# Retention attention and a GELU feed-forward on one core: v of chunk 2 moved to SyncE's queue, casts of chunk 2's k blocks two tiles later

## The chip, the core and the metric

The kernel runs on one core of a Trainium2 chip. Five engines work on their own instruction streams and wait for each other by semaphores: PE (TensorE, matmuls), DVE (VectorE), ACT (ScalarE), POOL (GpSimd) and SP (SyncE, which here only issues DMAs). The metric is the device time of one execution in microseconds (us). Six executions of the kernel before took 213.31 to 215.12 us, median 214.15 us.

## What is computed

q, k and v are float32 of shape 4 x 8 x 768 x 64 (batches, heads, positions, width of a head). Each head keeps a 64 x 64 state that decays by a factor gamma of its own at each position:

```python
for t in range(S):
    state = gamma[None, :, None, None] * state + np.einsum('bhd,bhe->bhde', k[:, :, t], v[:, :, t])
    y[:, :, t] = scale * np.einsum('bhd,bhde->bhe', q[:, :, t], state)
```

The result, laid out as 3072 tokens of width 512, goes through a feed-forward layer: `h = x @ w_in` (512 to 2048), GELU in its tanh form, and `g @ w_out` (2048 to 512).

## The kernel before

**Chunks.** The 768 positions are cut into six chunks of 128 (c = 0 to 5). A chunk holds its 128 positions of all four batches, so 512 tokens. Within a chunk the recurrence is done as matrix products. For a batch b of chunk c the names in the code are: `mm_T`/`ev_T` make the transposed q and k (tile qkT), `mm_A`/`ev_A` the masked products of k and q (PE writes a_ps, DVE multiplies by the mask into a_sb, line 257), `mm_yc` and `mm_yi` the output (y_ps) from the state and from a_sb with v, `ev_Y` brings it into xT, and `mm_s`/`ev_S` update the state st. `att_T`, `att_S` and `att_AY` bundle these.

**Feed-forward.** `moe1` (one tile of 128 hidden channels by 512 tokens, four matmuls) and `moe1_two` (two tiles of channels by 256 tokens, eight matmuls) multiply xT by w_in into a bank h_ps (line 390), and ACT takes the GELU of it into g (line 406). There are two banks for h_ps, so PE can be two tiles ahead of ACT, and no more. The second product uses a Winograd-like scheme with seven products in place of eight: `w_sums` makes sums of weights, `g_sums` sums of g into the tiles s_g (four operations for one or two groups of rows, line 429; on POOL for chunks 1 to 4), and `units_w(c)` is a list of 14 units (seven products, two halves of the tokens each) of eight matmuls into o_ps (line 498). The fifth unit of the list (unit 4) is the first that reads s_g, all eight groups of s_g[2]. Units 11 and 13 end with the stores of the chunk's output, 512 KB each, issued by POOL (line 531).

**The order of the work is written out by hand.** `run(units, after)` issues the units one by one, and after unit i whatever `after[i]` lists. An engine executes its own instructions strictly in that order. Here the stage of chunk c with its `moe1` units is called M(c), and that with `units_w(c)` is W(c). M(1) is a `run` of 16 units of `moe1_two` (lines 784 to 806), W(1) a second one (lines 807 to 823). From chunk 2 on, M(c) and W(c) are one `run` of 16 + 14 units (lines 826 to 857). The attention of chunk c + 1 is slipped in between the units of chunk c.

**Transposes of q and k.** For chunks 2 to 5 q and k come into SBUF a second way as well: `load_blk` (line 106) loads a chunk in 16 DMAs of 64 KB as blocks of 32 x 32 (tiles q32 and kT32, pieces of 128 bytes), `prep_blk` casts one batch of it to float16 (line 172 on ACT, line 174 on POOL), and `ev_T` transposes it on DVE in one instruction (line 230). Each cast reads what all 16 DMAs wrote. q32 has two buffers, kT32 one. `load1` (line 100) loads one batch of q, k or v as rows (256 KB, pieces of 256 bytes); `prep1` casts and scales it (v on POOL, line 185; k on ACT, line 172). v32 and k32 have eight buffers each, taken in the order of the loads in the code.

**DMA issue.** `load(c)` (line 117) is what SP issues for chunk c: q blocks, v (for c > 2), k blocks, then the rows of k. `load(2)` stands at line 738, behind a DMA of a table (line 737) that waits for POOL's line 736; `load(3)` stands after unit 8 of M(1), `load(4)` after unit 0 of M(2), `load(5)` after unit 0 of M(3). v of chunk 2 is issued by POOL, after unit 6 of the run that does W(0) (line 771). The weights, most of chunk 1's q, k and v, and nearly all stores of the output are issued by POOL too. In the profile q0 (software_dynamic) is POOL's DMA queue and q1 (hardware_dynamic) is SP's.

**The casts of the k blocks.** For chunk 2 ACT does them: batches 0 and 1 after units 8 and 10 of M(1), batches 2 and 3 in W(1). For chunk 3 ACT does them after units 8, 9, 11 and 13 of M(2) (line 844). For chunks 4 and 5 POOL does all four at the end of W(2) and W(3), behind the stores (line 856), and ahead of the g_sums of the next chunk.

Of the kernel before, what the change touches and what calls it, by code (L numbers as in the profile page):

```python
# [16 lines left out]
def kernel(  # L17
# [9 lines left out]
    nc = tc.nc  # L27
    B, H, S, Dh = q.shape
# [52 lines left out]
    def ld_all(key):  # L81
        if key not in raw:
            raw[key] = ld.tile(
                [128, B * NHP, 4, 32],
                F32,
                tag=key[0],
                bufs=2 if key[0] == "q32" else 1,
                name=key[0],
            )
        return raw[key]  # L90

    def ld_tile(nm, c, b):
        if nm == "q":
            t = ld_all(("q32", c)).rearrange("p (b hp) a d -> p b (hp a d)", b=B)
            return t[:, b].rearrange("p (h d) -> p h d", h=H)
        if (nm, c, b) not in raw:
            raw[nm, c, b] = ld.tile([128, H, Dh], F32, tag=f"{nm}32", bufs=8, name=f"{nm}32")
        return raw[nm, c, b]

    def load1(eng, nm, c, b):  # L100
        eng.dma_start(  # L101
            out=ld_tile(nm, c, b),
            in_=srcs[nm][b, :, c * C:(c + 1) * C, :].rearrange("h p d -> p h d"),
        )

    def load_blk(nm, c):
        t = ld_all((nm + ("32" if nm == "q" else "T32"), c))
        src = srcs[nm].rearrange("b (hp j) s (dd d) -> j dd s (b hp) d", j=2, dd=2)
        for j in range(2):
            for dd in range(2):  # L110
                for a in range(4):
                    p0, t0 = (2 * j + dd) * 32, c * C + a * 32
                    nc.sync.dma_start(  # L113
                        out=t[p0:p0 + 32, :, a, :], in_=src[j, dd, t0:t0 + 32]
                    )

    def load(c):
        load_blk("q", c)
        if c > 2:
            for b in range(B):  # L120
                load1(nc.sync, "v", c, b)
        load_blk("k", c)
        for b in range(B):
            load1(nc.sync, "k", c, b)

# [528 lines left out]
    VE, AC, PO, SY = nc.vector, nc.scalar, nc.gpsimd, nc.sync  # L654
# [81 lines left out]
    nc.gpsimd.tensor_copy(out=dec[0:1, 0, 0:1], in_=w_out_sb[3][0:1, 0, 0:1])  # L736
    nc.sync.dma_start(out=dec.rearrange("p h t -> p (h t)"), in_=dec_h.ap())
    load(2)
    for nm, b in ("q3", "k3", "v2", "v3"):
        load1(PO, nm, 1, int(b))  # L740
# [19 lines left out]
    def mm_Y(b, tag):  # L760
# [7 lines left out]
            1: [(w_sums, 3)],  # L768
            3: [(prep_qk, 1, 0)],
            5: [(att_T, 1, 0), (prep1, PO, "v", 1, 0), (prep1, PO, "v", 1, 1)],  # L770
            6: [(prep_qk, 1, 1)] + [(load1, PO, "v", 2, b) for b in range(B)],
            7: [(att_1A, 0)],
            8: [(att_T, 1, 1)],
            9: [(prep_qk, 1, 2)],
# [20 lines left out]
            5: [(mm_Y, 3, "o"), (ev_Y, 1, 3)],  # L795
            7: [(g_sums, PO, 1, 4, 8, 0, 1)],
            6: [(att_S, 1, 3), (prep_blk, AC, "q", 2, 0)],
            8: [(prep_blk, AC, "k", 2, 0), (load, 3)],
            9: [(prep_blk, AC, "q", 2, 1)],
            10: [(att_T, 2, 0), (prep_blk, AC, "k", 2, 1)],  # L800
            11: [(g_sums, PO, 1, 0, 4, 1, 2)],
            12: [(att_T, 2, 1)],
            14: [(att_AY, 1, (), "o", 2, (0, 1), None), (prep1, PO, "v", 2, 0), (prep1, PO, "v", 2, 1)],
            15: [(g_sums, PO, 1, 4, 8, 1, 2), (prep1, PO, "v", 2, 2), (prep1, PO, "v", 2, 3)],
        },
    )
    run(
# [18 lines left out]
    for c in range(2, NCk):  # L826
# [24 lines left out]
        if m < NCk:  # L851
            more(0, (load, m))
            for b in range(B):
                more((20, 21, 23, 24)[b], (prep_blk, AC, "q", m, b))
                more(24, (prep1, PO, "v", m, b))
                more(29, (prep_blk, PO, "k", m, b))
# [31 lines left out]
```

## Time and profile before

| | us |
|---|---|
| median of six executions | 214.15 |
| the profiled execution | 215.12 |
| its span, first to last instruction | 213.1 |
| time around the span | 2.0 |
| PE busy | 199.8 (94% of the span) |
| POOL busy | 130.0 (61%) |
| DVE busy | 111.1 (52%) |
| ACT busy | 106.1 (50%) |

A timeline line gives the start, the duration, the engine, the line of the kernel, the operation, output and inputs by the program's names, and how many instructions were merged; in brackets stands how long the engine had been idle before it, and what ended that. For SP the lines are the issue of DMAs, so their duration is the time that issuing took, and data lands later (a median of 2.8 us after the issue for a k block, of 5.3 us for a batch of k rows on SP). A line of a waits view reads "engine line <- what it waited for: us in total, times, longest". The windows view gives for each stretch the busy time of each engine with the number of instructions in brackets, then the granted PE clock, the DMA engines' share and GB/s. The lines of DMA queues give packets, MB and share of the 16 DMA engines.

### The profile page before, as it was taken

What the parts mean: (1) busy time and instruction counts of PE and PEld (TensorE: products, weight loads), DVE (VectorE), ACT (ScalarE), POOL (GpSimd) and SP (SyncE); (2) the same over time, 40 slices, a digit from 0 to 9 for tenths busy, and PEclk for the clock granted to TensorE, in tenths of its full rate; (3) what the DMA queues carried; (4) which work ended last, traced back from release to release, by engine and by line L of the source; (5) the groups of instructions that cost most, each with busy time, mean ns of one, the idle gap of its engine ahead of it and who ended that gap; (6) DMA issues with size and microseconds to landing.
All of it is one profiled execution on the core that took longest, in us unless ns stands there. A gap on an engine that the chain in (4) does not pass through costs nothing.

```text
span 213.1 us, 4854 instructions
## 1 busy us (share of the span) xinstructions
PE 199.8 (94%) x1948; PEld 137.2 (64%) x1948; DVE 111.1 (52%) x230; ACT 106.1 (50%) x189; POOL 130.0 (61%) x136
## 2 busy tenths in 40 slices
PE   5789999999991999999999999999999999999993
PEld 1447747777781788854478844588844688644883
DVE  3336489488541288820768740657730956134421
ACT  2375575355453474457874156655166631367321
POOL 0599335956295699528999379999289991200000
PEclk9999999999998599999999999999999999999999
DMA  7999999999878879779879799697891000310005
GB/s 163 287 253 207 206 207 298 328 293 238 196 123 165 164 123 208 113 186 276 126 144 192 112 253 233 102 218 119 139 311 38 0 3 3 143 54 0 3 0 198
DMA packets 117302, 34.24 MB, mean 161 GB/s; under 512 B 109984, under 2 KB 114464, under 8 KB 117280
## 3 DMA queue, kind: packets, MB, share of 16 engines
q1 hardware_dynamic: 103808, 18.21, 45.3%
q0 software_dynamic: 6944, 13.63, 24.2%
q10 hardware_dynamic: 6528, 2.10, 3.9%
q8 instruction: 15, 0.25, 0.5%
q14 instruction: 7, 0.06, 0.1%
HBM read 31.83 MB, written 6.29 MB: 179 GB/s over the span
## 4 chain that ended last, share of the span: by engine, by line
PE 66%; SPq 13%; DMA 11%; DVE 3%; POOL 3%; issue 1%; ACT 1%; ACTq 0%
PE h_ps L390 30%; PE o_ps L498 29%; SPq L113 12%; DMA w_out<-in_moe_w_out_dram 6%; DMA k<-in_k_dram 3%; PE y_ps L281 2%; PE y_ps L268 2%; PE a_ps L244 2%; DVE t_w L429 2%; DMA kT<-in_k_dram 2%; DVE s_g L429 1%; POOL w_in L371 1%; POOL k L185 1%; SPq L101 1%; PE s_ps L305 1%
## 5 line engine op out<-in xcount | busy, mean ns | idle before, releaser
L390 PE MATMUL h_ps<-xT,w_in 128*128 128x512 f16 (+2 forms) x488 | 90.2, 342 | 4.9 <-ACT g L406 4.9
L406 ACT ACTIVATE g<-h_ps 128x512 f16<-128x512 f32 (+1 forms) x98 | 57.4, 588 | 35.1 <-PE h_ps L390 34.6
L390 PEld LDWEIGHTS <-w_in 128*128 128x128 f16 x488 | 46.8, 100 | 43.2 <-issue 7.4
L257 DVE TENSOR_TENSOR a_sb<-a_ps,mask 128x512 f16<-128x512 f32 x48 | 30.1, 684 | 27.8 <-PE a_ps L244 27.8
L429 POOL TENSOR_TENSOR s_g<-g 128x512 f16<-128x512 f16 x32 | 36.9, 1152 | 12.4 <-ACT g L406 12.4
L498 PEld LDWEIGHTS <-s_g 128*128 128x128 f16 x320 | 30.2, 98 | 4.3
L498 PE MATMUL o_ps<-t_w,s_g 128*128 128x256 f16 x240 | 27.8, 273 | 0.0
L498 PEld LDWEIGHTS <-g 128*128 128x128 f16 x240 | 23.5, 98 | 3.5
L230 DVE STREAM_TRANSPOSE qkT<-kT 128x512 f16<-128x512 f16 x16 | 10.9, 683 | 21.3 <-ACT kT L172 15.7
L185 POOL TENSOR_TENSOR v<-v,cst 128x512 f16<-128x512 f32 x20 | 20.3, 1040 | 0.0
L429 POOL TENSOR_TENSOR s_g<-s_g,g 128x512 f16<-128x512 f16 x16 | 18.5, 1153 | 1.3
L429 POOL TENSOR_TENSOR s_g<-g,s_g 128x512 f16<-128x512 f16 x16 | 18.4, 1153 | 0.0
L531 POOL DMA_DIRECT2D out_dram<-o_sb x8 | 5.9, 736 | 20.5 <-DVE o_sb L429 16.9
L498 PE MATMUL o_ps<-w_out,g 128*128 128x256 f16 x160 | 18.3, 273 | 0.0
L297 DVE TENSOR_TENSOR xT<-y_ps,dec 128x512 f16<-128x512 f32 x20 | 13.1, 687 | 6.3 <-PE y_ps L281 6.3
L527 ACT COPY o_sb<-o_ps 128x512 f32<-128x512 f32 (+1 forms) x5 | 2.7, 543 | 25.0 <-PE o_ps L498 25.0
L429 DVE TENSOR_TENSOR s_g<-g 128x512 f16<-128x512 f16 x16 | 6.7, 421 | 12.6 <-ACT g L406 12.6
L172 ACT CAST q<-q 128x512 f16<-128x512 f32 x20 | 12.0, 619 | 2.4 <-DMA q<-in_q_dram 2.4
L172 ACT CAST k<-k 128x512 f16<-128x512 f32 x20 | 11.6, 619 | 0.1
L230 DVE STREAM_TRANSPOSE qkT<-q 128x512 f16<-128x512 f16 x16 | 11.1, 692 | 0.8 <-ACT q L172 0.7
L322 DVE SCALAR_TENSOR_TENSOR st<-st,cst,s_ps 128x128 f16<-128x128 f16 (+1 forms) x40 | 10.0, 316 | 0.5 <-PE s_ps L305 0.5
L521 ACT COPY s_u<-o_ps 128x512 f32<-128x512 f32 (+1 forms) x6 | 3.1, 514 | 14.2 <-PE o_ps L498 7.4
(68 smaller groups left out, 207.3 us busy)
## 6 DMA issues: line engine op xcount, KB each, us to landing
out_dram<-o_sb POOLq DMA_DIRECT2D x10, 512.0 KB, 4.8
k<-in_k_dram SPq DMA_DIRECT2D x18, 256.0 KB, 5.3
q<-in_q_dram SPq DMA_DIRECT2D x64, 64.0 KB, 3.0
kT<-in_k_dram SPq DMA_DIRECT2D x64, 64.0 KB, 2.8
v<-in_v_dram SPq DMA_DIRECT2D x14, 256.0 KB, 4.2
w_in<-in_moe_w_in_dram POOLq DMA_DIRECT2D x4, 512.0 KB, 8.7
w_out<-in_moe_w_out_dram POOLq DMA_DIRECT2D x4, 512.0 KB, 13.9
v<-in_v_dram POOLq DMA_DIRECT2D x8, 256.0 KB, 6.8
```

Source lines behind the costliest of these rows:

```text
L113: nc.sync.dma_start(out=t[p0:p0 + 32, :, a, :], in_=src[j, dd, t0:t0 + 32])
L172: eng.copy(out=out, in_=in_)
L185: eng.tensor_tensor(out=t, in0=src, in1=cst[:, col:col + H].unsqueeze(2).broadcast_to([128, H, Dh]), op=ALU.mult,)
L230: nc.vector.transpose(out=t[:, i].rearrange("p hp t -> p (hp t)"), in_=blk16.pop((nm, c, b)).rearrange("p ha d -> p (ha d)"),)
L257: nc.vector.tensor_tensor(out=s, in0=ps[j], in1=mask[:, j], op=ALU.mult)
L297: nc.vector.tensor_tensor(out=x, in0=ps, in1=dec, op=ALU.mult)
L322: nc.vector.scalar_tensor_tensor(out=t[:, :, hp], in0=t[:, :, hp], scalar=cst[:, OG + hp:OG + hp + 1], in1=s_ps[:, :, hp], op0=ALU.mult, o ...
L390: nc.tensor.matmul(out=out, lhsT=w_in_sb[wi][:, kc, wr * 128:(wr + 1) * 128], rhs=xT[c][:, kc, t0:t1], start=(kc == 0), stop=(kc == NHP - ...
L406: nc.scalar.activation(out=out, in_=in_, func=AF.Gelu_apprx_tanh, scale=1.0)
L429: eng.tensor_tensor(out=out, in0=in0, in1=in1, op=op)
L498: nc.tensor.matmul(out=po, lhsT=lhs(c, lk, fp, a), rhs=rhs(rk, fp), start=(new and fp == 0 and (last or a == 0)), stop=(stop and fp == NP ...
L531: eng.dma_start(out=rows[b, c * C:(c + 1) * C, a0:a1, n0:n1], in_=o_sb[b][:, a0:a1, n0:n1])
```

## The change

Three things are edited. `load(2)` issues v of chunk 2 itself, behind the k blocks and ahead of the k rows, and POOL no longer issues it. In M(1) the casts of the k blocks of batches 0 and 1 move from units 8 and 10 to units 10 and 11, their transposes from units 10 and 12 to 11 and 13, and the cast of q's batch 1 from unit 9 to unit 8. The products of k and q of these two batches (`att_AY` with an empty first list) move from unit 14 to unit 15, the last of M(1); POOL's order of work stays the same apart from the four DMA issues.

```diff
     def load(c):
         load_blk("q", c)
+        if c == 2:
+            load_blk("k", c)
+        for b in range(B):
+            load1(nc.sync, "v", c, b)
         if c > 2:
-            for b in range(B):
-                load1(nc.sync, "v", c, b)
-        load_blk("k", c)
+            load_blk("k", c)
         for b in range(B):
             load1(nc.sync, "k", c, b)
...
-            6: [(prep_qk, 1, 1)] + [(load1, PO, "v", 2, b) for b in range(B)],
+            6: [(prep_qk, 1, 1)],
...
-            8: [(prep_blk, AC, "k", 2, 0), (load, 3)],
-            9: [(prep_blk, AC, "q", 2, 1)],
-            10: [(att_T, 2, 0), (prep_blk, AC, "k", 2, 1)],
-            11: [(g_sums, PO, 1, 0, 4, 1, 2)],
-            12: [(att_T, 2, 1)],
-            14: [(att_AY, 1, (), "o", 2, (0, 1), None), (prep1, PO, "v", 2, 0), (prep1, PO, "v", 2, 1)],
-            15: [(g_sums, PO, 1, 4, 8, 1, 2), (prep1, PO, "v", 2, 2), (prep1, PO, "v", 2, 3)],
+            8: [(prep_blk, AC, "q", 2, 1), (load, 3)],
+            10: [(prep_blk, AC, "k", 2, 0)],
+            11: [(att_T, 2, 0), (prep_blk, AC, "k", 2, 1), (g_sums, PO, 1, 0, 4, 1, 2)],
+            13: [(att_T, 2, 1)],
+            14: [(prep1, PO, "v", 2, 0), (prep1, PO, "v", 2, 1)],
+            15: [(att_AY, 1, (), "o", 2, (0, 1), None), (g_sums, PO, 1, 4, 8, 1, 2), (prep1, PO, "v", 2, 2), (prep1, PO, "v", 2, 3)],
```

The loads stand earlier in the code now, so the eight buffers of v32 are handed out in another order: v of chunk 3, batches 2 and 3, takes the buffers of v of chunk 2, batches 0 and 1, where it took buffers of chunk 1 before.

## The prediction

> **What bounds the kernel now.** I began with the page's forty slices. PE is busy nearly everywhere but has one hole, and the granted clock falls once, just behind it.
>
> ```profile
> PE   5789999999991999999999999999999999999993
> ...
> PEclk9999999999998599999999999999999999999999
> ```
>
> PE shows a 1 in the thirteenth slice, 64 to 69 us; the clock is lowest in the fourteenth. The PE timeline and the waits view, cut to that stretch, say what it is:
>
> ```profile
> 60.40 3.67 PE L390 MATMUL h_ps<-xT,w_in 128*128 128x256 f16 x32
> 68.51 6.34 PE L390 MATMUL h_ps<-xT,w_in 128*128 128x256 f16 x32 [4.45 <-ACT g L406]
> ```
>
> ```profile
> PE h_ps L390 <- ACT g L406: 4.4, 1, 4.4
> ACT kT L172 <- DMA kT<-in_k_dram: 4.4, 1, 4.4
> ```
>
> ACT stands at the cast of chunk 2's k blocks, kT(2), until the last block lands at 67.17. The GELUs are queued behind that cast, PE uses up its two banks and stops. It pays twice: 4.45 us of idle time, and 32 matmuls in 6.34 us where the same 32 took 3.67 just before, because the clock had dropped. That is **7.1 us**. Elsewhere PE hardly waits.
>
> Why the blocks are late is in SP's issue timeline (how long each row took to issue):
>
> ```profile
> 37.16 18.25 SPq L113 DMA_DIRECT2D q<-in_q_dram  x16
> 55.45 8.73 SPq L113 DMA_DIRECT2D kT<-in_k_dram  x16
> 64.22 4.11 SPq L101 DMA_DIRECT2D k<-in_k_dram  x4
> 68.51 9.25 SPq L113 DMA_DIRECT2D q<-in_q_dram  x16
> 77.87 3.61 SPq L101 DMA_DIRECT2D v<-in_v_dram  x4
> 81.58 10.99 SPq L113 DMA_DIRECT2D kT<-in_k_dram  x16
> 92.67 6.53 SPq L101 DMA_DIRECT2D k<-in_k_dram  x4
> ```
>
> Row follows row without a gap from 37 us on, and load(4) goes on at 99.25. This stream is a second pacemaker beside PE: what is added to it makes everything behind later. That decides my forecast.
>
> **The change, part by part.**
>
> *v(2) leaves POOL's queue: S.* The DMA view for 42 to 56 us, when both queues are fed (packets, MB, share):
>
> ```profile
> q0 software_dynamic: 840, 2.84, 60.9%
> q1 hardware_dynamic: 6679, 0.83, 39.3%
> ```
>
> SP's queue alone moves about 1000 packets per us (6133 in 71 to 77 us). So 6679 packets are worth 6.7 of the 14 us, and 7.3 us went to 2.84 MB of POOL's, 0.39 MB/us. v(2) is 1.05 MB, 2.7 us. Lower bound 2.2: three of SP's q issues from 45.5 to 51 took 1.61, 1.49 and 1.70 instead of 0.49 us, 3.3 together, less 1.1 which the store's own share costs (the issue at 52.70 took 1.57). Upper bound 3.0, at the 0.35 MB of q0 alone in 36 to 37 us. So kT(2) lands at 67.17 - 2.7 = **64.5**. POOL saves 3.55 us of issuing, worth nothing: it then waited 3.2 us for DVE's output before its store.
>
> *The cast two tiles later.* ACT reached it at 62.95. Now a q cast (0.5 net) and two GELUs come first, the second bound by PE's unit 10, done at 64.07; ACT gets to the cast at about 64.65. kT(2) is there, by 0.2 us. At S = 2.2 ACT waits 0.4, which the two banks mostly cover. The stall goes.
>
> *What is late next in W(1).* POOL's g_sums waited for the stalled GELUs from 66.75 to 71.09, so POOL gains only 4.3 where PE gains 7.1. PE's first use of the last s_g[2] stood at 82.37 with the tile ready at 80.03: 75.3 against 75.7 now, 0.3 to 0.4 us lost. The k-q products one unit later are the same PE work; DVE's four mask products (2.5 us) then end about 0.9 us later relative to W(1), and the four transposes behind them just meet the products that need them. PE is **6.8 us** early at the end of W(1). The moved q and kT casts are the same instructions, 0.6 us each.
>
> *v(2) enters SP's queue: V.* Four DMAs of 1024 packets at 1000 per us, 4.1 us; v(3) took 3.7 us from first issue to the next row, v(4) and the first k block behind it 5.0. I take 4.3, bounds 3.7 and 5.0. SP's rows behind it are later by V - S = **1.6 us** (0.7 to 2.8). The k rows of chunk 2 come 1.6 later (the last landed at 72.0) but are cast at 72.9 and 77; v(2) itself lands by 70, POOL wants it at 71.3; the changed buffers make v(3) wait for POOL casts done by 73.4, SP is there at 80. None of these binds.
>
> The Trainium skill, "DMA: Bandwidth & Descriptors", section "Issuing engines are not separate DMA queues", says that whoever issues, the transfers run on the same 16 engines and only issue time differs. By it V = S and the 1.6 goes out of every sum below, leaving the total at about nothing instead of +1.75; the rows (0.39 MB/us on q0 against 0.25 on q1 for rows of 256 bytes) speak against it.
>
> *kT(3), the next cast that ACT can stand at.*
>
> ```profile
> 100.38 0.60 ACT L406 ACTIVATE g<-h_ps 128x512 f16<-128x512 f32 x1 [0.35 <-PE h_ps L390]
> 100.87 0.61 ACT L172 CAST kT<-kT 128x512 f16<-128x512 f32 x1
> ```
>
> Before, its last block was issued at 92.08 and landed 3.4 later, at 95.5: 5.4 us to spare. Now ACT is there at 100.87 - 6.8 = 94.1, and the blocks are later twice over. First V - S, 1.6. Second, W(1)'s two stores: they were issued at 91.65 and 93.29, behind the kT(3) blocks, and cost the k rows instead. From 93 to 99 us q1 moved 3099 packets where it moves 6000, so 2.9 us went to the stores. Now they come at about 88.2 and 89 (POOL has v(3), landing at 87.0, to cast first), while SP is issuing kT(3) until 94. I take 2.5 (1.8 to 2.9). kT(3) lands at 95.5 + 1.6 + 2.5 = **99.6** (98.0 to 101.2).
>
> As at the first stall, PE starts 1.34 us after the landing (68.51 - 67.17): 100.95. Before, it began unit 11 of M(2) at 102.3 (two tiles of 0.87 ahead of 104.06). So 1.35 us remain of 6.8, after PE stood idle from 95.5 on, 5.45 us. A hole of 4.45 cost 2.7 us of slow clock in this trace; this one is longer, so I charge **2.7** again: PE leaves M(2) 1.3 us later than before.
>
> "TensorE: Matmul & The Clock Gate" of the same skill, Part 1, says that the clock falls after an idle window of some 3.4 us, and that these windows run freely. An estimate from it: a hole of 5.45 holds a whole window in about 6 of 10 cases; in the rest the sum here would be 1.35 early instead of 1.3 late. The one hole in this trace fell with 4.45.
>
> *kT(4), cast on POOL.*
>
> ```profile
> 122.57 0.75 POOL L531 DMA_DIRECT2D out_dram<-o_sb  x1 [3.59 <-DVE o_sb L429]
> 124.21 0.72 POOL L531 DMA_DIRECT2D out_dram<-o_sb  x1 [0.89 <-ACT o_sb L527]
> 125.07 2.28 POOL L174 CAST kT<-kT 128x512 f16<-128x512 f32 x4
> 127.53 1.15 POOL L429 TENSOR_TENSOR s_g<-g 128x512 f16<-128x512 f16 x1 [0.17 <-ACT g L406]
> ...
> 142.46 1.15 POOL L429 TENSOR_TENSOR s_g<-s_g,g 128x512 f16<-128x512 f16 x1
> ```
>
> The blocks landed at 124.66, the casts began at 125.07, and the g_sums then run without a pause to 143.61, where PE reads that s_g at about 143.7 in W(3). The slack is 0.4 + 0.15 + 0.1, **0.65 us**; beyond that PE pays one for one. Now kT(4) lands at 126.3; the stores, 1.3 later with PE, end at 126.2. POOL is then as late as PE, with 0.4 for the tail that meets the stores. Behind that chunk 5's blocks have 0.8 us of slack and PE is late itself: nothing.
>
> Sum: -6.8 + 5.45 + 2.7 + 0.4 = **+1.75 us**. The profiled execution, 215.12 (span 213.1 and 2.0 around it), becomes 216.9; from the median of 214.15, which it exceeds by 1.0, **215.9**. With the bounds of kT(3), 98.0 to 101.2, the same case runs from 214.2 to 217.5.
>
> **The rivals.**
>
> *SP keeps up: faster.* q1 is not full everywhere (463 and 656 packets in 84 to 86 us); if v(2) goes into such holes and the stores share better, kT(3) lands at about 96.8, PE is idle 2.65 us, the clock stays, and 4.1 us remain: 210.0. If nothing waits, 6.8: 207.3. It decides where kT(3) lands before 98.3 with the clock dropping, and only while kT(4) lands before 125.3. Against it: SP's rows leave no gap and the stores now precede both block loads.
>
> *It cancels: same.* V - S at 0.7, or a clock drop half as long: within 1.07 us (0.5%, about what a measurement of this kernel can tell from no change) of 214.15.
>
> *The clock holds in M(2), and POOL pays: slower by more.* PE being 1.35 early, W(2)'s stores meet the last kT(4) blocks, which lose 1.5 to 2.5 us and land at 127.8 to 128.8. POOL starts its casts there, and PE waits in W(3): 2.5 to 3.5 later than before, and 2.7 more if that hole drops the clock. 216.7 to 220.
>
> *The change doesn't do what it says.* If S were 0, kT(2) still lands at 67.17, PE stops for 2.6 us and is 4.2 early, kT(3) lands near 102 and the clock drops: 3.5 later, 217.7.
>
> **Chances.** Forecast 0.42, cancelling 0.21, faster 0.22, POOL pays 0.10, doesn't do it 0.05. Slower by over 0.5% has 0.42 + 0.15 = 0.57, same 0.21, faster 0.22. The range from 211.0 to 218.5 leaves out the better part of the faster case (0.13) and the worst of the slow ones (0.06).
>
> **What would show it.** Right: no hole at 64 to 69 us and kT(2) at 64 to 65; SP begins q of chunk 3 at about 70.1; ACT waits at kT(3) for some 5 us near 95 to 99.6, with PE's hole and a clock drop behind it. Wrong: q of chunk 3 begins at 68.5 or before, kT(3) lands before 98, or the PE row has no second hole. POOL pays if its wait moves to the kT casts at 126 to 129 and PE waits for s_g in W(3).

## The result, and the profile after

The changed kernel took 219.57 us in the median of 21 executions (215.38 to 221.39), the kernel before on the same chips 214.05 (47 executions). The ratio, here and below, leaves out executions more than 1.5% above the fastest of their kernel, which are 13 of the 21 of the changed kernel: with the rest the ratio to before is 1.0137 (95% interval 1.0104 to 1.017), or 217.0 us. The forecast of 215.9 has the direction; the size was larger. The 217.0 lies within the range that was forecast (211.0 to 218.5), the median of all 21 above it. The profiled execution took 221.23 us (span 219.5), close to the longest of all, and its trace speaks for that one alone.

The page's slices of the changed kernel (PE busy share, granted clock):

```profile
PE   4889999999997999956999999929999999999993
...
PEclk9999999999999999996999999996999999999999
```

The 1 in the thirteenth slice is gone. In its place stand two holes, at about 95 to 104 us and at 143 to 148, each with a clock drop behind it. The PE timeline names what ended them (line numbers are two higher than before):

```profile
67.09 2.91 PE L392 MATMUL h_ps<-xT,w_in 128*128 128x256 f16 x24 [1.58 <-ACT g L408]
100.56 3.38 PE L392 MATMUL h_ps<-xT,w_in 128*128 128x512 f16 x8 [4.23 <-ACT g L408]
148.10 3.61 PE L500 MATMUL o_ps<-t_w,s_g 128*128 128x256 f16 x18 [4.17 <-POOL s_g L431]
```

The first is what is left of the old stall, the second is kT(3), the third POOL's s_g in W(3). The waits view gives the causes of the last two, a landing each time (the view names k rows for POOL, but the cast reads kT, whose last block landed at 129.50; the k rows, queued behind it, landed from 130.26 on):

```profile
ACT kT L174 <- DMA kT<-in_k_dram: 4.1, 1, 4.1
POOL kT L176 <- DMA k<-in_k_dram: 4.8, 1, 4.8
```

SP's rows, with v(2) as the second:

```profile
51.35 10.99 SPq L113 DMA_DIRECT2D kT<-in_k_dram  x16
62.38 3.94 SPq L101 DMA_DIRECT2D v<-in_v_dram  x4
66.38 4.00 SPq L101 DMA_DIRECT2D k<-in_k_dram  x4
70.56 10.19 SPq L113 DMA_DIRECT2D q<-in_q_dram  x16
80.89 3.68 SPq L101 DMA_DIRECT2D v<-in_v_dram  x4
84.67 12.61 SPq L113 DMA_DIRECT2D kT<-in_k_dram  x16
```

Before, q of chunk 3 began at 68.51 and kT(3) at 81.58; now 2.1 and 3.1 us later, and kT(3) takes 12.61 instead of 10.99. W(1)'s stores, issued at 90.45, now fall on it. At the end of M(2) PE is exactly where it was: W(2) begins at 107.16 against 107.15. Nearly all of the loss of this execution arises in W(3), where POOL stands at kT(4):

```profile
122.59 0.75 POOL L533 DMA_DIRECT2D out_dram<-o_sb  x1 [3.66 <-DVE o_sb L431]
124.23 0.72 POOL L533 DMA_DIRECT2D out_dram<-o_sb  x1 [0.89 <-ACT o_sb L529]
129.71 2.28 POOL L176 CAST kT<-kT 128x512 f16<-128x512 f32 x4 [4.75 <-DMA k<-in_k_dram]
131.97 1.14 POOL L431 TENSOR_TENSOR s_g<-g 128x512 f16<-128x512 f16 x1
```

The stores stand where they stood (122.57 and 124.21). The casts behind them start at 129.71 instead of 125.07, the g_sums follow without a pause, and PE resumes at 148.10.

### The profile page after: what moved, and what is told of

The parts are those of the page before. It is cut to its first block, busy times and chain, and to the rows that moved or that the text cites. A ratio compares the mean times of both kernels' runs of the same rounds, so it can differ in the third digit from the quotient of the medians.

```text
span 219.5 us, 4856 instructions
## 1 busy us (share of the span) xinstructions
PE 200.8 (91%) x1948; PEld 137.0 (62%) x1948; DVE 110.8 (50%) x230; ACT 106.5 (49%) x189; POOL 127.2 (58%) x132
## 4 chain that ended last, share of the span: by engine, by line
PE 51%; SPq 21%; DMA 12%; POOL 5%; DVE 4%; ACT 2%; issue 2%; ACTq 0%; POOLq 0%
PE h_ps L392 23%; PE o_ps L500 23%; SPq L113 20%; DMA w_out<-in_moe_w_out_dram 5%; DMA k<-in_k_dram 3%; POOL s_g L431 3%; DVE t_w L431 2%; DVE s_g L431 2%; DMA v<-in_v_dram 2%; PE y_ps L270 2%; PE a_ps L246 1%; PE y_ps L283 1%; DMA q<-in_q_dram 1%; DMA kT<-in_k_dram 1%; POOL k L187 1%
## 5 line engine op out<-in xcount | busy, mean ns | idle before, releaser
L392 PE MATMUL h_ps<-xT,w_in 128*128 128x512 f16 (+2 forms) x488 | 89.0, 337 | 6.3 <-ACT g L408 6.3
L392 PEld LDWEIGHTS <-w_in 128*128 128x128 f16 x488 | 45.8, 98 | 44.1 <-issue 9.9
L500 PEld LDWEIGHTS <-s_g 128*128 128x128 f16 x320 | 30.8, 100 | 9.4 <-POOL s_g L431 4.6
L500 PE MATMUL o_ps<-t_w,s_g 128*128 128x256 f16 x240 | 29.5, 281 | 4.2 <-POOL s_g L431 4.2
L431 POOL TENSOR_TENSOR s_g<-s_g,g 128x512 f16<-128x512 f16 x16 | 18.4, 1153 | 1.3
```

The source lines that it names most:

```text
L392: nc.tensor.matmul(out=out, lhsT=w_in_sb[wi][:, kc, wr * 128:(wr + 1) * 128], rhs=xT[c][:, kc, t0:t1], start=(kc == 0), stop=(kc == NHP - ...
L431: eng.tensor_tensor(out=out, in0=in0, in1=in1, op=op)
L500: nc.tensor.matmul(out=po, lhsT=lhs(c, lk, fp, a), rhs=rhs(rk, fp), start=(new and fp == 0 and (last or a == 0)), stop=(stop and fp == NP ...
```

## The experiments

Theory 1 is the prediction's: v(2) lengthens SP's stream, the blocks behind it come late, and PE pays where a cast of such blocks stands in an engine's order ahead of what PE needs. Theory 2: the new order of M(1) is what costs. Theory 3: SP plays no part; whenever PE is early, its stores move ahead of the block loads, and that gives the gain back. Ratios are to the kernel before, measured beside it, with 95% intervals.

**The two halves of the change.** The order alone keeps `before`'s `load` and POOL's issue of v(2); the load alone keeps M(1)'s old table.

```diff
 order_only (against after)
+            6: [(prep_qk, 1, 1)] + [(load1, PO, "v", 2, b) for b in range(B)],
 load_only (against before): load(c) as in the change, and
-            6: [(prep_qk, 1, 1)] + [(load1, PO, "v", 2, b) for b in range(B)],
+            6: [(prep_qk, 1, 1)],
```

> v of chunk 2 stays on POOL as before, only M(1)'s order is changed. Theory 1 (SP's stream is longer by V - S, and everything behind v(2) on it comes late): SP's rows stand as before (q of chunk 3 issued from about 68.5), kT(2) lands at about 67.2, the hole in M(1) shrinks from 4.45 to about 2.6 us with little or no clock drop, and the time is 1 to 3 us below before, 211 to 213. Theory 2 (the new order of M(1) itself costs): as slow as the changed kernel, 217. Theory 3 (SP plays no part: whenever PE is early, the stores of W(1) and W(2) move ahead of the block loads and give the gain back): 214 or more, with kT(4) landing 2 us or more later than before.

> v of chunk 2 on SP behind the k blocks, M(1)'s order as before. Theory 1: SP's rows as in the changed kernel (q of chunk 3 from about 70.5), kT(2) lands at 65 to 66, so ACT, there at 63, waits about 3 us and a hole of 2.5 to 3.5 us stays in M(1); kT(3) and kT(4) land as late as in the changed kernel, PE waits for s_g in W(3), 216 to 218. Theory 2: no loss without the new order, 214 or below. Theory 3: PE is less early, so the stores collide less: between before and the changed kernel, 215.

The order alone: 0.9887 (0.9817 to 0.9956). The load alone: 1.0137 (1.0081 to 1.0194), the ratio of the whole change. The PE timelines of the two, order first:

```profile
67.35 2.91 PE L390 MATMUL h_ps<-xT,w_in 128*128 128x256 f16 x24 [2.03 <-ACT g L406]
138.56 2.14 PE L498 MATMUL o_ps<-t_w,s_g 128*128 128x256 f16 x18 [0.19 <-POOL s_g L429]
```

```profile
65.48 3.92 PE L392 MATMUL h_ps<-xT,w_in 128*128 128x256 f16 x32 [0.84 <-ACT g L408]
101.25 3.57 PE L392 MATMUL h_ps<-xT,w_in 128*128 128x512 f16 x8 [4.64 <-ACT g L408]
```

With v(2) on POOL the stall of M(1) shrinks to 2.0 us without a clock drop, and kT(3) is there when ACT comes for it (no wait at 95.42), although the stores fall on it there too. With v(2) on SP the M(1) stall almost goes, but the hole at kT(3) comes. This kernel shows the forecast's own case nearly alone, with POOL on time at 126.39, and its profiled execution is 1.8 us longer in span than before's (214.9 against 213.1). The time is the expected one; the place is not quite: I expected a hole of 2.5 us or more to stay in M(1), and POOL to be late in W(3). Theory 2 falls.

**The order alone, run again.**

> The new order of M(1) alone once more, v of chunk 2 on POOL. Theory 1: kT(4) lands at 120 to 125 by chance of how the stores meet it, and PE's wait in W(3) is its landing plus 18.4 us: between 210 and 216.5 from run to run as in the first look, on average 0.5 to 1.5% below before. If the first look was luck: no difference from before or slower.

0.9951 (0.9903 to 0.9999), 210.07 to 217.72 us. The profiled execution took 216.06 us, and it shows a wait that the profile of the first run lacks:

```profile
123.46 2.28 POOL L174 CAST kT<-kT 128x512 f16<-128x512 f32 x4 [4.15 <-DMA kT<-in_k_dram]
...
141.86 4.02 PE L498 MATMUL o_ps<-t_w,s_g 128*128 128x256 f16 x18 [3.65 <-POOL s_g L429]
```

SP's issue of kT(4) took 11.06 us here and 9.69 in the first run, in the same kernel. So theory 3 holds in part: with PE 5.6 us early the stores of W(2) (116.95 and 118.59) precede the end of kT(4), and the gain stands or falls with how they meet. The mean of all twelve executions, 213.87 us, is that of the kernel before beside them (213.85), so a lasting gain of the order alone isn't shown. But theory 3 isn't the whole cause of the change's loss: the stores come so early in this kernel too, and the mean of the changed kernel's executions is 218.98.

**How much of the loss is POOL's wait.** The casts of kT(4), then of kT(4) and kT(5), go from POOL to ACT as chunk 3's already are.

```diff
 kT4_on_ACT and, on the kernel before, before_kT4_ACT (after_kT45_ACT: for every c, and POOL's line deleted)
-                if c == 2:
+                if c in (2, 3):
                     more((8, 9, 11)[b], (prep_blk, AC, "k", n, b))
-                more(((9, 10, 13) if c == 2 else (6, 8, 13))[b], (att_T, n, b))
-            if c == 2:
+                more(((9, 10, 13) if c in (2, 3) else (6, 8, 13))[b], (att_T, n, b))
+            if c in (2, 3):
                 more(13, (prep_blk, AC, "k", n, 3))
...
-                more(29, (prep_blk, PO, "k", m, b))
+                if m != 4:
+                    more(29, (prep_blk, PO, "k", m, b))
```

> The changed kernel, but the four casts of chunk 4's k blocks are done by ACT in M(3) after units 8, 9, 11 and 13, as those of chunk 3 are in M(2); POOL's g_sums of chunk 3 no longer stand behind them. Theory 1: kT(4) lands as late as in the changed kernel (about 129) but nobody waits for it: the hole in W(3) goes, and the time falls by 3 to 5 us, to 212 to 214; the hole at kT(3) stays. Theory 2: no change, 217. Theory 3: as theory 1 here.

> The kernel before with chunk 4's k blocks cast by ACT in M(3), as a control for the same edit on the changed kernel. Theory 1: before had 0.65 us of slack there, so nothing is gained: 213.5 to 214.5. If that edit were an improvement of its own that has nothing to do with late blocks: 1% or more faster, 212 or less.

> The changed kernel with the k blocks of chunks 4 and 5 cast by ACT in M(3) and M(4) after units 8, 9, 11 and 13; POOL casts none. Theory 1: neither W(3) nor W(4) has a hole any more, what remains of the loss is the hole at kT(3) (3.5 to 4.5 us and a slow clock) against the one saved in M(1): 213 to 215. If the loss lay elsewhere: as the version with chunk 4 alone, 215.6 or more.

On the changed kernel 1.0052 (1.0022 to 1.0082) with kT(4) and 1.0024 (0.9972 to 1.0075) with both; on the kernel before 0.9985 (0.9951 to 1.0019). The edit helps only where the blocks are late. With kT(4) alone, 215.62 us is above the 212 to 214 I expected, in part because a hole of 1.39 us opened in W(4):

```profile
156.81 2.28 POOL L176 CAST kT<-kT 128x512 f16<-128x512 f32 x4 [1.88 <-DMA kT<-in_k_dram]
...
175.20 4.76 PE L500 MATMUL o_ps<-t_w,s_g 128*128 128x256 f16 x42 [1.39 <-POOL s_g L431]
```

With both, a single hole is left, at kT(3):

```profile
99.44 3.24 PE L392 MATMUL h_ps<-xT,w_in 128*128 128x512 f16 x8 [3.91 <-ACT g L408]
```

That hole with its slow clock (3.9 and 1.5 us) eats most of the 7.1 that M(1) gained, and POOL's casts are the loss on top. The medians fall with them: 219.57 us for the changed kernel, 215.62 and 214.61 here, while the same edit leaves the kernel before where it was (213.20 against 213.5).

**Without the stores of chunks 1 and 2** (they are left out of the output).

```diff
-                    if n > 4:
+                    if n > 4 and c not in (1, 2):
                         store(n - 5, 0, 2, 0, d_model, nc.gpsimd)
```

> The changed kernel without the four stores of the output of chunks 1 and 2 (left out of the output). Theory 1 with the stores' share as predicted: kT(3) lands about 2.5 us earlier than in the changed kernel, at 96 to 97, kT(4) at 127 or before since only V - S is left, the hole in W(3) shrinks to 2 us or less, and the time falls to 212 to 215. If V - S alone were the cause: kT(3) stays at about 99, kT(4) at about 129, 217. Theory 3: both blocks land as in the kernel before or earlier, and the time falls below before, to 209 to 211.

0.9952 (0.9918 to 0.9986).

```profile
96.41 2.03 PE L392 MATMUL h_ps<-xT,w_in 128*128 128x512 f16 x8 [0.60 <-ACT g L408]
140.90 3.54 PE L500 MATMUL o_ps<-t_w,s_g 128*128 128x256 f16 x18 [2.69 <-POOL s_g L431]
```

ACT casts kT(3) at 95.24 instead of 99.39, 4 us earlier: SP comes to its row 1.0 us earlier, and the row is 3.2 us shorter (9.43 against 12.61). Not all of that is the stores' doing. In the changed kernel the first block of the row alone took 2.49 us, and the stores were issued only later, at 90.45. Behind them four blocks took 0.80, 0.55, 1.42 and 1.34 us instead of 0.49. That is a share of some 2.1 us, where I took 2.5. Yet kT(4) is still too late for POOL, by 8.2 us of waiting, and W(3) keeps a hole of 2.7 where I expected 2 or less. So no store is needed for that hole once PE is early: SP's row of kT(4) ends 2.6 us later than in order_only (120.24 against 117.62), with v(2) on SP as the other difference.

**Half of v(2) on SP.**

```diff
-        for b in range(B):
+        for b in range(B if c > 2 else 2):
             load1(nc.sync, "v", c, b)
...
+            6: [(prep_qk, 1, 1)] + [(load1, PO, "v", 2, b) for b in (2, 3)],
```

> The changed kernel with only half of v(2), batches 0 and 1, on SP; batches 2 and 3 stay on POOL where they were. Theory 1: SP's rows behind it are late by half as much, q of chunk 3 issued from about 69 (67.4 with none, 70 to 70.5 with all four), kT(3) lands at 97 to 98 and the time lies between the order alone (212.2) and the changed kernel, 213 to 216. If it were the place of the first v behind the k blocks that mattered and not the amount: as the changed kernel, 217 or more.

1.0146 (1.0033 to 1.0259) and a median of 218.0 us, a miss: as far as four executions tell, half the load costs as much as the whole. That is the time expected if the place of v(2) mattered and not the amount, but the trace doesn't bear that out. SP's q of chunk 3 begins at 68.86, and ACT finds kT(3) landed at 95.20, so the hole at kT(3) is gone. But PE, 5.6 us early there, meets kT(4), whose issue took 11.54 us among the stores:

```profile
124.27 2.28 POOL L176 CAST kT<-kT 128x512 f16<-128x512 f32 x4 [4.98 <-DMA kT<-in_k_dram]
...
142.65 4.02 PE L500 MATMUL o_ps<-t_w,s_g 128*128 128x256 f16 x18 [4.17 <-POOL s_g L431]
```

This is the hole of order_only_5 (3.65 us), where nothing of v(2) is on SP. The loss doesn't grow in step with SP's delay: one hole closes and another opens. In all six kernels whose W(3) waits for POOL, PE resumes 18.4 us after POOL begins the kT(4) casts (2.3 of casts, 16.1 of g_sums):

| kernel | casts of kT(4) begin | PE resumes in W(3) |
|---|---|---|
| changed kernel | 129.71 | 148.10 |
| order_later (below) | 124.48 | 142.88 |
| v_half | 124.27 | 142.65 |
| order_only_5 | 123.46 | 141.86 |
| no_stores_12 | 122.50 | 140.90 |
| order_only | 120.16 | 138.56 |

**Casts later still, and off POOL.** Three steps, all with v(2) on POOL: order_later puts the k casts of M(1) after units 12 and 13; all_later also casts kT(3) and kT(4) on ACT after units 10 to 13; all_ACT does so for kT(5) as well. The fourth run is all_ACT with `load` as in the change.

```diff
 order_later (against order_only)
-            10: [(prep_blk, AC, "k", 2, 0)],
-            11: [(att_T, 2, 0), (prep_blk, AC, "k", 2, 1), (g_sums, PO, 1, 0, 4, 1, 2)],
-            13: [(att_T, 2, 1)],
+            11: [(g_sums, PO, 1, 0, 4, 1, 2)],
+            12: [(prep_blk, AC, "k", 2, 0)],
+            13: [(att_T, 2, 0), (prep_blk, AC, "k", 2, 1)],
+            14: [(att_T, 2, 1), ...
 all_ACT (all_later: for c = 2 and 3 only)
-            12: [(att_AY, n, (), "att", n, (0, 1), None)],
+            14: [(att_AY, n, (), "att", n, (0, 1), None)],
...
+                more((10, 11, 12)[b], (prep_blk, AC, "k", n, b))
+                more((11, 12, 13)[b], (att_T, n, b))
+            more(13, (prep_blk, AC, "k", n, 3))
...
-                more(29, (prep_blk, PO, "k", m, b))
```

> v of chunk 2 on POOL, the new order of M(1), and the two k casts there two tiles later still (units 12 and 13, transposes after 13 and 14). Theory 1: ACT comes to kT(2) at about 66.5, the remaining hole of 2.0 us in M(1) falls to 1 or less, PE is up to 6.5 us early at the end of W(1), and ACT then reaches kT(3) at about 94, shortly before it lands: the time falls by another 0.5 to 1.5 us against the order alone, 210.5 to 211.7, with a wait at kT(3) of 1 us or less. If late transposes held up the products: no gain, 212 or more.

> As the run with the casts later still, and in M(2) and M(3) the casts of the next chunk's k blocks by ACT after units 10 to 13, their transposes one unit behind, the first products after unit 14 instead of 12; POOL casts chunk 5's blocks only. Theory 1: neither kT(3) nor kT(4) is waited for; what is left is PE's own work and at most 1 us at kT(2): 208.5 to 211, unless a late product of k and q holds PE at the end of M(2) or M(3), which would show as PE waiting for DVE's transposes there: 212 or more.

> v of chunk 2 on POOL, ACT casts the k blocks of chunks 3, 4 and 5 after units 10 to 13 of the stage before (transposes one unit behind, first products after unit 14), those of chunk 2 after units 12 and 13 of M(1); POOL casts none. Theory 1 (PE waits only where a cast of late blocks stands in its way): the last hole, that of W(4) with 3.5 us and its slow clock (5 us together), goes, and the time falls by about 5 us against the kernel that still left chunk 5 to POOL, to 208 to 210.5, 1.5 to 3% below before. If PE is held by something else at that pace: 212 or more.

> The kernel with all k casts on ACT and later, with one difference: v of chunk 2 on SP behind the k blocks, as in the changed kernel. Theory 1: SP's rows behind it are 2 to 3 us later than without, kT(3) lands at about 99 and ACT, there at about 96, waits some 3 us; the time is 1 to 4 us above the same kernel with v on POOL. If v on SP costs nothing by itself once POOL's casts are gone: no difference between the two.

order_later: 1.0065 (1.0026 to 1.0105) and 215.59 us, a miss against 210.5 to 211.7. The hole in M(1) falls to 0.45 us as expected, but ACT then waits 2.7 us at kT(3) and POOL 2.3 at kT(4):

```profile
98.13 3.18 PE L390 MATMUL h_ps<-xT,w_in 128*128 128x512 f16 x8 [2.82 <-ACT g L406]
```

So an earlier PE can lose by itself, with nothing added to SP. That again is theory 3 in part, and a part of the change's loss may be of this kind.

all_later: 0.9962 (0.9915 to 1.0009) and 214.23 us, a miss against 208.5 to 211. Apart from 0.93 us in M(1) the only hole left is in W(4), 3.49 us with a slow clock behind it, where POOL still casts kT(5). all_ACT: **0.9837** (0.9777 to 0.9897), 209.54 us, faster than both kernels. In its profile PE waits for a cast once:

```profile
68.75 1.03 PE L390 MATMUL h_ps<-xT,w_in 128*128 128x256 f16 x8 [0.55 <-ACT g L406]
```

The same kernel with v(2) on SP: 0.9949 (0.9911 to 0.9986), 212.18 us, 2.6 more, in the range expected. SP's q of chunk 3 begins at 71.86 instead of 68.24, and PE waits for ACT at q and kT of chunk 3:

```profile
88.14 9.72 PE L392 MATMUL h_ps<-xT,w_in 128*128 128x512 f16 x44 [1.56 <-ACT g L408]
99.84 2.03 PE L392 MATMUL h_ps<-xT,w_in 128*128 128x512 f16 x8 [1.98 <-ACT g L408]
```

This pair is the cleanest price of the moved load. It also bears on the rule of "DMA: Bandwidth & Descriptors", section "Issuing engines are not separate DMA queues", that only issue time depends on the issuer, and that it is usually small. Issuing v(2) took 3.55 us on POOL before and 3.94 on SP in the changed kernel. POOL had the time, for it waited 3.2 us behind it; SP's rows follow without a gap for over 100 us, so there such a sum is not small. How much of SP's time is its own issuing, and how much the sharing of the DMA engines, no run separates.

## Why the prediction was right, and where it was off

- **SP is the second pacemaker, and v(2) on it costs more than it frees.** Right in kind; load_only and the all_ACT pair show it. In size V was 4.0 us (4.3 predicted), but S too large: kT(2) landed at 65.75 and not at 64.5, so S is 1.4 us, not 2.7, and below my lower bound of 2.2. Between 42 and 62 us SP's queue moved 14187 packets in the changed kernel, 13309 in order_only and 12402 before, 0.9 to 1.8 us' worth. Freed DMA time isn't SP's for the taking: without v(2) it issues a block every 0.53 us at best, and W(0)'s stores fall on its blocks all the same. q of chunk 3 begins 2.1 us later than in the kernel before. In all seven profiles with v(2) on POOL it begins at 67.4 to 68.6 (68.2 in the mean), in all six with the whole of it on SP at 69.9 to 72.1 (70.9). So V - S is about 2.7 instead of 1.6, at my upper bound of 2.8.
- **The stall of M(1)** was to go; 1.58 us of it stayed, without a clock drop, because of S. PE began M(2) 5.7 us early, not 6.8.
- **kT(3)**: landed at 99.25 (predicted 99.6), PE back at 100.56 (100.95). Right by luck, as the errors made up for each other: SP came to the row 3.1 us late instead of 1.6, the row was 1.6 us longer instead of 2.5, and the last block landed 2.45 us after its issue. For that I had read 3.4 and a landing at 95.5 in the trace before, which is the middle of the last two blocks; the last took 3.9 and landed at 95.97. The slow clock behind the hole cost 1.6 us (8 matmuls in 3.38 us, against some 1.75 at full clock), not 2.7: the granted clock was 0.50 for 3.41 us here and for 6.8 us in M(1) before. PE left M(2) on time, not 1.3 late.
- **kT(4) is the term that was mis-sized most.** I charged 0.4 us, on the ground that PE would be late itself. With PE on time the stores came at their old time, kT(4)'s last block was issued 2.8 us later than before (124.42 against 121.66) and took 5.1 us to land instead of 3.2. That cost 4.2 us of idle PE and 1.5 of slow clock (18 matmuls in 3.61 us, 2.14 in order_only), nearly all of the 6.4 us by which this span is longer. The place and the mechanism are those of the rival "the clock holds in M(2), and POOL pays", to which I gave a chance of 0.10, though its condition wasn't met: the clock did fall in M(2). Of the signs that I named, the forecast's (a wait at kT(3) with a hole and a clock drop behind it) and this rival's (a wait at the casts of kT(4), 129.71 where I named 126 to 129, and PE waiting for s_g in W(3)) both came.
- **What stays open.** Only this execution of the changed kernel was profiled, so which of the others have the hole in W(3) isn't known. That the hole also comes in shorter executions is seen in v_half (217.66 us) and no_stores_12 (213.85). That the forecast's path alone can give the 2.9 us of the ratio is seen in load_only, whose four executions took 215.28 to 217.94 us and whose profile has no hole in W(3); whether it did so in the changed kernel isn't shown.

## What to carry to other kernels

When a stall goes, look for the next consumer of the same stream, not of the same engine: here every block load was a deadline (kT(2), kT(3), kT(4), kT(5)), and an earlier PE met the next one. A strictly ordered engine that waits for a transfer holds back all that stands behind it, so the waiting instruction belongs as late in that order as its user allows, and on the engine whose successors can wait. Here moving a load between queues was priced by the pace of the queue that received it: 4.0 us for v(2) on SP, against the 1.4 us by which kT(2) landed earlier without it on POOL's queue.

## What the runs showed of the hardware

Between 60 and 200 us, matmuls ran slow behind every hole of PE of 2.69 us or more (2.69, 2.82, 3.49, 3.56, 3.65, 3.91, 4.17, 4.17, 4.20, 4.23, 4.45, 4.64) and at full speed behind all those from 1.39 to 2.35 us (1.39, 1.47, 1.56, 1.56, 1.58, 1.72, 1.79, 1.98, 2.03, 2.35). But the length of a hole alone doesn't decide. In the changed kernel the granted clock was 0.50 from 100.78 to 104.19 and from 148.57 to 151.98, 3.41 us each time, and the two starts lie 14 such steps apart. In order_later it fell at 97.37, inside the hole from 95.30 to 98.13. The windows view gives the steps around that, and the step of all_ACT_v_SP that holds its whole hole of 1.98 us; the granted clock is the third number from the end:

```profile
93.96:97.37 3.41, 1.34 (x6) 0.48 (x5) 0.00 (x0) 0.68 (x2) 3.33 (x4) 1.00 0.87 167
97.37:100.78 3.41, 2.65 (x7) 0.97 (x7) 1.90 (x3) 2.46 (x6) 1.78 (x3) 0.50 1.11 238
```

```profile
96.44:99.85 3.41, 1.43 (x8) 0.56 (x7) 0.53 (x1) 1.50 (x4) 3.33 (x4) 1.00 0.91 182
99.85:103.26 3.41, 3.41 (x29) 1.55 (x29) 3.41 (x7) 2.95 (x6) 3.33 (x4) 1.00 1.14 232
```

A step in which PE was busy for 1.34 us was followed by the slow clock, one with 1.43 us was not. "TensorE: Matmul & The Clock Gate", Part 1, gives an idle window of about 3.4 us, running freely. The steps of 3.41 us agree with that; that the window must be idle does not, for 2.07 us of idle time in it were enough here. How a hole lies to the steps counts as well, so a safe length of a hole isn't shown by these runs. The drops lasted one step or two and cost about 1.1 to 2.7 us.

One kernel's profile differed between two executions by 3.3 us in the landing of the same blocks (order_only and order_only_5, last block of kT(4) at 119.92 and 123.22), with stores at the same time within 0.2 us. Its issue was 1.2 us later (118.37 against 117.13), and it took 4.9 us to land instead of 2.8. What makes the difference isn't shown. A wait with no slack passes it on to PE, and that may be where the spread of the times comes from.
